# A windowed attention with a SiLU MLP behind it: seven products of quarters in one more group of tokens, and sums of weights that stay on the chip

## Chip, cores and metric

One core of a Trainium2 chip runs the whole program. The metric is device time in microseconds (us) of one launch, median of several runs. The kernel before takes 900.89 us.

## What is computed

Queries, keys and values have 8 batches, 8 heads, 576 positions and 64 columns per head. Attention is causal with a window of 128 positions and a linear bias per head. Its result is laid out as 4608 tokens of 512 columns, `x`, and goes through an MLP:

```
scores = q @ k.T / 8 - slope * distance        (0 <= distance < 128 only)
x      = softmax(scores) @ v                   4608 x 512
h      = x @ w_in                              4608 x 2048
out    = (h * sigmoid(h)) @ w_out              4608 x 512
```

All inputs are float32. The kernel keeps more than float16 precision by splitting each number into a high and a low float16 part and adding three matmuls: high*high, high*low, low*high.

## The kernel before

**Stages.** Tokens go in nine groups of 512, numbered g = 0 to 8 here as in the code (`NG`, `TG`); the "group 7 of nine" of the change's name is g = 6. The hidden width of 2048 is cut in 16 slices of 128 (`NF`), and n = 16*g + f counts group and slice. `gemm1(n, half)` makes a slice of `h`, `act1` to `act4` (L940 to L1009) make SiLU of it and split it in `gh` and `gl`, `gemm2(n, half)` adds its part of the output. Groups 0 and 1 work partly on float32 words; from group 2 on the MLP on TensorE is float16. The attention of later tokens is mixed into the MLP of earlier ones, in "pairs" (one tile of 128 tokens, four heads); nine pairs begin per group until the end of group 6, and groups 7 and 8 run with almost no attention beside them.

**The first and second product of a plain group** (2 to 6): `gemm1` (L897) issues 12 matmuls of 512 columns per slice, `gemm2` (L1114) 4 tiles * 3 = 12 of 512 columns, into the PSUM banks w, x, y, z (one per tile of 128 tokens), which `store` (L1135) empties at the group's end.

**Groups 7 and 8** (`FAST`, L81) work on half a group of tokens (256) and on two slices 1024 columns apart at a time, and take the second product from seven products of quarter matrices instead of eight (`gemm2_fast`, L1017). `gemm1_fast` (L885) issues 2 * 12 matmuls of 256 columns per n, `gemm2_fast` 7 * 3 = 21 of 256 columns. For it ACT and DVE make 7 blocks instead of 4 (`act_sums` L968, `act3` L977, `act4` L996: 896 columns in two instructions instead of 512 in one), and POOL makes sums of the quarters of `w_out` ahead of time (`sum_float`, `sum_make`, `sum_hi`, `sum_lo`, L699 to L744; scheduled from step 302 on, every 17 steps). `join_products` and `add_corners` (L1087, L1068) put the products together from the PSUM banks. In group 8 (`SEVEN`) the first product is taken from seven products too (`gemm1_seven`, L853), with sums of the quarters of `w_in` (`in_float` to `in_lo`, L775 to L796). These are made on POOL and ACT in groups 2 to 4, six of eight are stored to HBM (`in_away`, L756) and loaded again in groups 6 and 7 (`in_back`, L761).

**Order.** The order on each engine is written out by hand. The program is a list of steps; one step is one `gemm1` or `gemm2` half (in group 8 a third of the first product). `plan` holds, by step number, what else is emitted ahead of that step's matmuls: attention, splits, sums. Engines run in that order, and SP's DMA queue issues in it too. `gemm2` of n follows `gemm1` by a lag:

```
left = LAG + (n >= SEVEN * NF - 1) if g in FAST else 1
if f == NF - 1 and (g not in FAST or g == NG - 1):
    left = 0
```

So in plain groups `gemm2` runs one n behind and catches up at the group's end, in groups 7 and 8 it runs 3 behind. A pair p that begins at step n has `scores` at n (PE, into the two PSUM banks a), `row_max` at n+1 (DVE, L526), `exps` at n+2 and n+3 (ACT, L541), `p_hi` (ACT, L551) and `p_lo` (POOL, L557) at n+3 to n+5, a DMA that transposes the halves (`hl`, L567), and `attend` (PE, L609) at n+11, again into a bank a, which `normalize` (DVE, L622 to L638) empties. Pairs begin 7 steps apart.

The scales of batches 4 and 5 and of 6 and 7 come from a chain of four stages (`vscale_finish`, `scales16`, L294), whose last stage is a small matmul on PE (L325). For the last batches the stages stand at steps 268, 271, 273 and 275 (`FINISH`, L66).

Of the kernel before, what the change touches and what calls it, by code (L numbers as in the profile page):

```python
# [121 lines left out]
def tile_window_attention_then_silu_mlp(ctx, tc, qk, v, w_in, w_out, distance, out):  # L122
# [623 lines left out]
    win, piece, away = {}, {}, {}  # L746

    def in_pieces(j):

        both = [pool.tile([P, 2, DM], F32, tag="big", name=f"wb{j}_{k}") for k in range(2)]  # L750
        piece["r"] = [both[0][:, s] for s in range(2)]
        piece["q"] = [both[1][:, s].rearrange("p (s c) -> p s c", s=2) for s in range(2)]
        w = pool.tile([P, 2, 4, DM // 2], F16, tag=IN_TAGS[j] if j < 2 else AWAY[j % 2], bufs=1, name=f"wx{j}")
        win[j] = [w[:, part] for part in range(2)]

    def in_away(j):  # L756
        away[j] = dram.tile([P, 2, 4, DM // 2], F16, name=f"away{j}")
        for part in range(2):
            nc.sync.dma_start(away[j][:, part], win[j][part])

    def in_back(j):  # L761
        if j in IN_TAGS:
            w = pool.tile([P, 2, 4, DM // 2], F16, tag=IN_TAGS[j], bufs=1, name=f"wy{j}")
            win[j] = [w[:, part] for part in range(2)]
        elif j < HALF_F - 1:
            tag, bufs = ("q", 2) if j < 4 else ("x", 4)
            w = [pool.tile([P, 4, DM // 2], F16, tag=tag, bufs=bufs, name=f"wy{j}_{part}") for part in range(2)]
            win[j] = [a[:] for a in w]
        else:
# [11 lines left out]
    def in_make(j, k):
        (a11, a12), (a21, a22) = ([r[:, h * DM // 2 : (h + 1) * DM // 2] for h in range(2)] for r in piece["r"])
        one, two = piece["q"]
        if k == 0:
            nc.gpsimd.tensor_add(one[:, 0], a21, a22)
            nc.gpsimd.tensor_sub(one[:, 1], one[:, 0], a11)
# [300 lines left out]
    def join_products(g, t, half):  # L1087

        scale = gsc[g][:, 2:3]
        if half == 0:  # L1090
            both = pool.tile([P, 2, 2, DM // 2], F32, tag="w1_6", bufs=1, name=f"of{g}_{t}")
            st["out"] = [both[:, k] for k in range(2)]
            st["once"] = once = pool.tile([P, 2, DM // 2], F32, tag="rv", bufs=2, name=f"once{g}_{t}")
            nc.scalar.activation(once.rearrange("p a c -> p (a c)"), ops[1], AF.Copy, scale=scale)
# [445 lines left out]
```

## Time and profile before

| | before |
|---|---|
| median of 3 runs | 900.89 us (900.48 to 901.05) |
| the profiled execution: its time | 901.33 us |
| its span, first to last instruction | 899.5 us |
| PE busy | 99% of the span |
| DVE, ACT, POOL busy | 68%, 68%, 46% |
| group 6 (first matmul of 6 to first of 7) | 644.26 to 741.61 us |
| group 7 (to the first matmul of group 8) | 741.61 to 811.76 us |

The profile records each instruction with its engine, line, tiles and duration. A matmul's duration is its passage through the array, so that neighbours overlap; how fast PE goes is read from the starts of successive blocks. A group of instructions gives the line, the engine, the operation, output<-inputs, the shape, the count, then busy us, mean ns of one, and the idle time of the engine ahead of them with what ended it.

### The profile page before, as it was taken

The numbers are of one execution on the slowest core, as the hardware profiler recorded it, in microseconds if no ns is written. First come the engines' busy times: TensorE is split into PE (matmuls) and PEld (weight loads), VectorE is DVE, ScalarE is ACT, GpSimd is POOL, SyncE is SP. The second block draws the span as 40 slices with busy tenths as digits, with TensorE's granted clock in tenths as the row PEclk, the third lists the DMA queues.
The fourth block names the chain that finished last, engine by engine and source line by source line (L and its number), as shares of the span: only waits on it lengthen the run. The fifth ranks groups of instructions, "written<-read, shape, count | busy, mean of one in ns | idle before, by whom it ended". The sixth has DMA issues, their size and how long they took to land. (4 is left out here: it accounts for less than half of the span.)

```text
span 899.5 us, 20129 instructions
## 1 busy us (share of the span) xinstructions
PE 891.8 (99%) x7657; PEld 592.2 (66%) x7657; DVE 611.3 (68%) x1591; ACT 613.3 (68%) x1336; POOL 411.5 (46%) x462
## 2 busy tenths in 40 slices
PE   9999999999999999999999999999999999999998
PEld 7877777888855555455554454455555558889997
DVE  6998988677866766555766665556665557776665
ACT  7789986776578856878865676656676754435553
POOL 2356652233333326566665775657466721003441
PEclk9999999999999999999999999999999999999999
DMA  8989924345479743878674647343663246310000
GB/s 301 402 204 230 274 56 134 71 94 95 106 205 224 204 95 89 228 175 212 142 176 118 129 106 147 89 96 81 135 145 85 60 107 162 85 37 7 20 26 24
DMA packets 206160, 120.98 MB, mean 134 GB/s; under 512 B 170864, under 2 KB 173040, under 8 KB 206064
## 3 DMA queue, kind: packets, MB, share of 16 engines
q1 hardware_dynamic: 205632, 119.31, 53.1%
q8 instruction: 60, 0.98, 0.5%
q10 hardware_dynamic: 432, 0.39, 0.1%
q14 instruction: 36, 0.29, 0.1%
HBM read 65.67 MB, written 12.58 MB: 87 GB/s over the span
## 5 line engine op out<-in xcount | busy, mean ns | idle before, releaser
L1130 PE MATMUL o<-w,gh 128*128 128x512 f16 (+1 forms) x896 | 273.6, 387 | 0.1
L920 PE MATMUL h<-xt,w 128*128 128x512 f16 (+1 forms) x1344 | 269.7, 349 | 0.0
L557 POOL TENSOR_TENSOR hr<-t,hr 128x512 f16<-128x512 f32 (+1 forms) x108 | 119.7, 1121 | 253.3 <-ACT hr L551 170.7
L920 PEld LDWEIGHTS <-w 128*128 128x128 f16 x1344 | 126.3, 98 | 112.3 <-issue 3.3
L961 DVE SCALAR_TENSOR_TENSOR h<-gt,h 128x512 f32<-128x512 f32 x112 | 77.8, 694 | 159.9 <-ACT gt L955 159.6
L1130 PE MATMUL o<-w,gl 128*128 128x512 f16 (+1 forms) x448 | 172.0, 384 | 0.2
L955 ACT ACTIVATE gt<-h,tsc 128x512 f32<-128x512 f32 x112 | 76.3, 681 | 92.9 <-PE h L920 79.5
L1130 PEld LDWEIGHTS <-gh 128*128 128x128 f16 x640 | 59.3, 98 | 66.7
L526 DVE CUSTOM_DVE_ANT_0 t<-sp,tab 128x256 f32<-128x256 f32 (+1 forms) x288 | 99.9, 401 | 1.9 <-PE sp L502 1.3
L551 ACT ACTIVATE hr<-t 128x512 f16<-128x512 f32 (+1 forms) x128 | 74.1, 598 | 2.6 <-DMA hl<-hr 2.6
L541 ACT ACTIVATE t<-t,mx,vsc 128x256 f32<-128x256 f32 (+1 forms) x144 | 74.8, 578 | 1.2
L1007 DVE SCALAR_TENSOR_TENSOR gl<-h,gh 128x512 f16<-128x512 f32 x80 | 55.0, 687 | 24.2 <-ACT gh L993 23.8
L541 ACT ACTIVATE t<-t,mx 128x256 f32<-128x256 f32 (+1 forms) x144 | 61.8, 488 | 4.5 <-DVE mx L526 3.8
L993 ACT ACTIVATE gh<-h 128x512 f16<-128x512 f32 x80 | 47.2, 590 | 22.4 <-DVE h L961 22.1
L609 PEld LDWEIGHTS <-hl 128*128 128x128 f16 x1464 | 52.0, 98 | 15.8 <-issue 4.5
L171 POOL TENSOR_TENSOR x<-xs,x 128x256 f16<-128x256 f32 x54 | 39.1, 725 | 43.5 <-ACT x L648 43.3
L609 PE MATMUL av<-v,hl 128*128 128x65 f16 (+1 forms) x1464 | 55.4, 193 | 0.9 <-DVE mx L526 0.6
L1130 PEld LDWEIGHTS <-gl 128*128 128x128 f16 x320 | 31.3, 98 | 37.9 <-DVE gl L1007 0.3
L1130 PEld LDWEIGHTS o<-w,gh 128*128 128x128 f32 x256 | 45.6, 188 | 10.0 <-issue 0.5
L925 PE MATMUL h<-xh,w 128*128 128x512 f32 x128 | 44.5, 404 | 0.0
L892 PE MATMUL h<-xt,w 128*128 128x256 f16 x384 | 44.2, 273 | 0.0
L171 POOL TENSOR_TENSOR w<-wm,w 128x512 fp32r<-128x512 f32 x32 | 43.0, 1343 | 2.6
(241 smaller groups left out, 1603.7 us busy)
## 6 DMA issues: line engine op xcount, KB each, us to landing
qs<-qk SPq DMA_DIRECT2D x18, 512.0 KB, 4.8
r<-qk SPq DMA_DIRECT2D x18, 512.0 KB, 4.4
wr<-w_in SPq DMA_DIRECT2D x16, 512.0 KB, 6.6
wr<-w_out SPq DMA_DIRECT2D x16, 512.0 KB, 6.5
rv<-v SPq DMA_DIRECT2D x30, 256.0 KB, 3.5
out<-ot SPq DMA_DIRECT2D x28, 256.0 KB, 3.0
vm<-v SPq DMA_DIRECT2D x27, 256.0 KB, 4.7
q<-qk SPq DMA_DIRECT2D x18, 256.0 KB, 3.9
```

What stands on the lines that cost most here:

```text
L171: engine.tensor_sub(out, a, b)
L526: nc.vector.tensor_tensor_reduce(out=st[p]["t"][u][:, h, 2 * P - n :], in0=st[p]["sp"][h][:, u, o].rearrange("p o c -> p (o c)"), in1=tab[ ...
L541: nc.scalar.activation(x, x, AF.Exp, bias=mx[:, 2 * u + h : 2 * u + h + 1], scale=scale)
L551: nc.scalar.activation(split_of(p, u, hr)[:, 0], t[:, :, 2 * P - n :], AF.Copy, scale=scale)
L557: nc.gpsimd.tensor_sub(hr[:, 1], t[:, :, 2 * P - n :], hr[:, 0])
L609: nc.tensor.matmul(av[:, 2 * u + h, : rhs.shape[-1]], lhs, rhs, start=(n == 0), stop=(n == len(seq) - 1), skip_group_check=True,)
L920: nc.tensor.matmul(o, w[:, wp, cc], x, start=start and k == 0, stop=stop, skip_group_check=True)
L955: nc.scalar.activation(gt, hps[n], AF.Tanh, scale=scale)
L961: nc.vector.scalar_tensor_tensor(out=h, in0=gt, scalar=1.0, in1=h, op0=ALU.add, op1=ALU.mult)
L993: nc.scalar.activation(gh, gt, AF.Copy, scale=cut_of(n))
L1007: nc.vector.scalar_tensor_tensor(out=gl, in0=gt, scalar=cut_of(n), in1=f32(gh) if n // NF < OUT16 else gh, op0=ALU.mult, op1=ALU.subtract)
L1130: nc.tensor.matmul(ops[ti], a[:, t], w, start=(f == 0 and i == 0), stop=(f == NF - 1 and i == len(seq) - 1), skip_group_check=True,)
```

## The change

Seven parts:

1. `FAST` takes in group 6. Its products go through `gemm1_fast` and `gemm2_fast`, its activations through the seven-block form; `act_sums` of group 6 stand on POOL (only those of group 7, `ALONE`, stay on DVE). Its `act3` stands 7 steps behind `gemm1` and its `act4` 8 (`ACT_LATE`, `ACT_LOW`); group 7 keeps 4 and 6.
2. The lag is 1, then 2 from slice 4, then 3 from slice 9 of group 5 (`lag_of`), so that groups 5 and 6 no longer catch up at their ends. Group 5 to 2 put `gh` and `gl` of one n into one tile, tags gh and gl in turn, which gives four n's room.
3. The sums of `w_out` begin at step 176 instead of 302, every 23 steps.
4. The sums of `w_in` for j = 0, 1 stand at steps 191 and 214, those for j = 2 to 7 at 453 to 503, in group 7. `in_away` and `in_back` are gone.
5. For pairs from 18 on, `p_lo` of the second half stands on DVE, `x_hi` and `x_lo` one step later; `v_hi` is two steps earlier and `v_lo` one later, `hi16` and `lo16` move by a step. The sums of x for group 8 are 5 steps later.
6. The four stages of the last scales stand at 268, 274, 281, 288.
7. Outputs of seven-product groups keep their first part in the output tile itself, without the tile `once`; group 6 writes them from two tiles q. Both halves of group 6 and the first half of group 7 add up in banks w, x, y, z; the order of products at a half's start follows.

```diff
-FINISH = {1: (37, 42, 45), 2: (166, 168, 169, 170), 3: (268, 271, 273, 275)}
+FINISH = {1: (37, 42, 45), 2: (166, 168, 169, 170), 3: (268, 274, 281, 288)}
-IN_SUMS = (186, 200, 214, 228, 242, 256, 270, 284)
-IN_BACK = {2: 440, 3: 444, 4: 460, 5: 468, 6: 474, 7: 480}
-AWAY = ("w1_7", "w1_8")
+SUMS, SUMS_STEP = 176, 23
+IN_GAP = 15
+IN_EARLY = (SUMS + IN_GAP, SUMS + SUMS_STEP + IN_GAP)
+IN_FIRST, IN_STEP = 453, 10
+IN_SUMS = IN_EARLY + tuple(IN_FIRST + IN_STEP * j for j in range(8 - len(IN_EARLY)))
-FAST = (NG - 2, NG - 1)
+FAST = (NG - 3, NG - 2, NG - 1)
+ALONE = NG - 2
-SUMS, SUMS_STEP = 302, 17
+RAMP = (4, 9)
+ACT_LATE = 7
+ACT_LOW = 1
+V_HI, V_LO = 7, 3
+P_HI = (3, 4)
+P_LO = (4, 5)
+X_OFF = 3
+LOW_DVE = 1
...
         if p >= LOW_POOL:
-            nc.gpsimd.tensor_sub(hr[:, 1], t[:, :, 2 * P - n :], hr[:, 0])
+            minus(nc.vector if u and LOW_DVE else nc.gpsimd, hr[:, 1], t[:, :, 2 * P - n :], hr[:, 0])
             return
...
-        engine, a = nc.gpsimd if n // NF == SEVEN else nc.vector, gact[n]
+        engine, a = nc.vector if n // NF == ALONE and n % NF >= ALONE_POOL else nc.gpsimd, gact[n]
...
-        gh = pool.tile([P, TG], dt, tag="gh", name=f"gh{n}")
-        gl = pool.tile([P, TG], dt, tag="gl", name=f"gl{n}")
+        if n // NF < OUT16:
+            gh, gl = (pool.tile([P, TG], dt, tag=tag, name=f"{tag}{n}") for tag in ("gh", "gl"))
+        else:
+            both = pool.tile([P, 2, TG], dt, tag=("gh", "gl")[n % 2], name=f"gb{n}")
+            gh, gl = both[:, 0], both[:, 1]
...
-        if j == 0 and g == SEVEN:
+        if j == 0 and g != ALONE:
             first = 3
...
-                    ops[b] = psum.tile([P, DM], F32, tag=("axaz" if t or g == SEVEN else "wxyz")[b], bufs=2 if (t or g == SEVEN) and b % 2 == 0 else 1, name=f"m{g}_{t}_{b}")
+                    free = g == SEVEN or g == ALONE and t
+                    tag = ("axaz" if free else "wxyz")[b]
+                    ops[b] = psum.tile([P, DM], F32, tag=tag, bufs=2 if tag == "a" else 1, name=f"m{g}_{t}_{b}")
...
-        if j > 1:
-            put(IN_SUMS[j] + 17, in_away, j)
-            put(IN_BACK[j], in_back, j)
...
+        def lag_of(n):
+            g, f = divmod(n, NF)
+            if n == NG * NF - 1 or f == NF - 1 and g + 1 < FAST[0]:
+                return 0
+            if g in FAST:
+                return LAG + (n >= SEVEN * NF - 1)
+            return 1 + (f >= RAMP[0]) + (f >= RAMP[1]) if g + 1 in FAST else 1
...
-                left = LAG + (n >= SEVEN * NF - 1) if g in FAST else 1
-                if f == NF - 1 and (g not in FAST or g == NG - 1):
-                    left = 0
+                left = lag_of(n)
```

## Rows read from the trace of the kernel before

**Rows 1.** The page: busy us, share of the span and instructions of each engine.

```profile
PE 891.8 (99%) x7657; PEld 592.2 (66%) x7657; DVE 611.3 (68%) x1591; ACT 613.3 (68%) x1336; POOL 411.5 (46%) x462
```

**Rows 2.** Groups 6 and 7: PE, PEld, DVE, ACT, POOL busy; clock, DMA share, GB/s.

```profile
644.26:741.61 97.35, 97.35 (x817) 49.39 (x816) 54.35 (x157) 64.30 (x127) 56.70 (x63) 1.00 0.47 109
741.61:811.76 70.15, 70.15 (x661) 62.95 (x660) 53.69 (x113) 28.65 (x50) 2.94 (x4) 1.00 0.35 91
```

**Rows 3.** Timeline of PE in group 6: start us, us, engine, line, count.

```profile
702.39 2.75 PE L920 MATMUL h<-xt,w 128*128 128x512 f16 x12
704.98 0.59 PE L1130 MATMUL o<-w,gh 128*128 128x512 f16 x2
```

**Rows 4.** Timeline of PE in group 7.

```profile
764.93 2.78 PE L892 MATMUL h<-xt,w 128*128 128x256 f16 x24
767.55 0.60 PE L1036 MATMUL m<-w,gt 128*128 128x256 f16 x4
...
769.84 2.78 PE L892 MATMUL h<-xt,w 128*128 128x256 f16 x24
```

**Rows 5.** What PE waited for from 250 us on: total us, times, longest.

```profile
PE vs L325 <- DVE mx L526: 0.8, 1, 0.8
PE av L609 <- DMA hl<-hr: 0.2, 1, 0.2
```

**Rows 6.** Timeline at 476 to 480 us, in group 4, the last scales.

```profile
476.72 1.46 PE L920 MATMUL h<-xt,w 128*128 128x512 f16 x6
...
479.00 0.35 PE L325 MATMUL vs<-row,ones 1*128 1x8 f32 x2 [0.82 <-DVE mx L526]
...
479.29 1.47 PE L920 MATMUL h<-xt,w 128*128 128x512 f16 x6
```

**Rows 7.** Groups of instructions by shape, group 6: DVE, ACT and POOL.

```profile
L1007 DVE SCALAR_TENSOR_TENSOR gl<-h,gh 128x512 f16<-128x512 f32 x16 | 11.0, 687 | 4.7 <-ACT gh L993 4.7
L443 DVE SCALAR_TENSOR_TENSOR packed<-r,vsc,packed 128x512 f16<-128x512 f32 x8 | 6.9, 865 | 0.0
...
L993 ACT ACTIVATE gh<-h 128x512 f16<-128x512 f32 x16 | 9.5, 593 | 6.9 <-DVE h L961 6.9
...
L557 POOL TENSOR_TENSOR hr<-t,hr 128x512 f16<-128x512 f32 x19 | 21.8, 1158 | 39.7 <-ACT hr L551 31.1 <-issue 8.3
```

**Rows 8.** The same, group 7: the seven-block split on DVE and on ACT.

```profile
L1000 DVE SCALAR_TENSOR_TENSOR gl<-gt,gh 128x640 f16<-128x640 f32 x7 | 5.7, 818 | 0.2 <-ACT gh L983 0.2
...
L1000 DVE SCALAR_TENSOR_TENSOR gl<-gt,gh 128x256 f16<-128x256 f32 x7 | 2.9, 417 | 0.0
...
L983 ACT ACTIVATE gh<-gt 128x640 f16<-128x640 f32 x7 | 5.1, 735 | 10.2 <-DVE gt L975 10.2
...
L983 ACT ACTIVATE gh<-gt 128x256 f16<-128x256 f32 x7 | 2.8, 400 | 0.0
```

**Rows 9.** POOL's sums over the whole span, by shape.

```profile
L779 POOL TENSOR_TENSOR wb<-w 128x512 f32<-128x512 f16 x16 | 18.9, 1185 | 0.0
...
L973 POOL TENSOR_TENSOR gt<-gt 128x256 f32<-128x256 f32 x7 | 5.1, 729 | 17.7 <-DVE gt L964 17.7
...
L975 POOL TENSOR_TENSOR gt<-gt 128x128 f32<-128x128 f32 x7 | 4.6, 663 | 0.5
```

**Rows 10.** Lines L559 and L443 on DVE: ns min/median/max, first and last start.

```profile
L559 DVE SCALAR_TENSOR_TENSOR hr<-t,hr x20: 669/681/1342, 48.0 to 150.0; 128x512 f16<-128x512 f32 x20
...
L443 DVE SCALAR_TENSOR_TENSOR packed<-r,vsc,packed x36: 731/746/1669, 349.8 to 716.3; 128x512 f16<-128x512 f32 x36
```

**Rows 11.** Timeline of a pair of attention in group 6, and median landing of its transposes.

```profile
698.49 2.27 POOL L557 TENSOR_TENSOR hr<-t,hr 128x512 f16<-128x512 f32 x2 [5.50 <-issue]
...
706.28 0.89 PE L609 MATMUL av<-v,hl 128*128 128x65 f16 x24
...
hl<-hr SPq DMA_TRANSPOSE x18, 2.7
```

**Rows 12.** DMAs that bring sums of w_in back: SP's issue time, ns, first and last.

```profile
L773 SPq DMA_DIRECT2D wy<-away x10: 371/424/533, 733.7 to 762.0; - x10
```

More of the change, by code (lines that the diff above doesn't have):

```diff
@@ L653, in x_lo @@
             cols = slice(q * 4 * D, (q + 1) * 4 * D)
-            minus(nc.gpsimd if p >= LOW_POOL else nc.vector, xt[i][:, 1, cols], st[p]["x"], xt[i][:, 0, cols])
+            minus(nc.gpsimd if p >= LOW_POOL and not X_DVE else nc.vector, xt[i][:, 1, cols], st[p]["x"], xt[i][:, 0, cols])
             if q == 1:
@@ L744, in sum_lo @@
         nc.gpsimd.tensor_sub(out16[:, 1], wsum["r"][:, 0, : DM // 2], out16[:, 0])
[L746 to L769, printed above, removed]
+    win, piece = {}, {}
@@ L770, in in_back, with in_tile @@
+    def in_tile(j):
+        if j == HALF_F - 1:
             flat = [a.rearrange("p s h d -> p (s h d)")[:, : 2 * DM] for a in (v1, v2)]
             win[j] = [a.rearrange("p (s c) -> p s c", s=4) for a in flat]
-        for part in range(2):
-            nc.sync.dma_start(win[j][part], away[j][:, part])
-    def in_float(j, k):
-        if k == 0:
-            in_pieces(j)
-        w = w16[0, j + k * HALF_F]
-        nc.gpsimd.tensor_add(piece["r"][k].rearrange("p (c f) -> p c f", c=NCC), w[:, 0], w[:, 1])
@@ L781, in in_make @@
[L781 to L786, printed above, removed]
-        else:
-            nc.gpsimd.tensor_sub(two[:, 0], a11, a21)
-            nc.gpsimd.tensor_sub(two[:, 1], a12, one[:, 1])
+            return
+        tag, bufs = IN_TAGS[j]
+        if bufs == 1:
+            w = pool.tile([P, 2, 4, DM // 2], F16, tag=tag, bufs=1, name=f"wx{j}")
+            win[j] = [w[:, part] for part in range(2)]
+        else:
+            w = [pool.tile([P, 4, DM // 2], F16, tag=tag, bufs=bufs, name=f"wx{j}_{part}") for part in range(2)]
+            win[j] = [a[:] for a in w]
@@ new lines, in in_float, with in_make @@
+    def in_float(j, k):
+        if j >= len(IN_EARLY):
+            piece[k] = pool.tile([P, DM], F32, tag="rv", bufs=2, name=f"wb{j}_{k}")
+        else:
+            if k == 0:
+                piece["room"] = pool.tile([P, 2, DM], F32, tag=IN_ROOM, bufs=1, name=f"wb{j}")
+            piece[k] = piece["room"][:, k]
+        r = piece[k]
+        w = w16[0, j + k * HALF_F]
+        nc.gpsimd.tensor_add(r.rearrange("p (c f) -> p c f", c=NCC), w[:, 0], w[:, 1])
+    def in_make(j, k):
+        (a11, a12), (a21, a22) = ([piece[k][:, h * DM // 2 : (h + 1) * DM // 2] for h in range(2)] for k in range(2))
+        if k == 0:
+            nc.gpsimd.tensor_add(a22, a21, a22)
+            nc.gpsimd.tensor_sub(a21, a11, a21)
+        else:
+            nc.gpsimd.tensor_sub(a11, a22, a11)
+            nc.gpsimd.tensor_sub(a12, a12, a11)
@@ L1090, in join_products @@
         if half == 0:
[L1091 to L1094, printed above, removed]
+            if g < ALONE:
+                st["out"] = [pool.tile([P, 2, DM // 2], F32, tag="q", bufs=2, name=f"of{g}_{t}_{k}") for k in range(2)]
+            else:
+                both = pool.tile([P, 2, 2, DM // 2], F32, tag="w1_6", bufs=1, name=f"of{g}_{t}")
+                st["out"] = [both[:, k] for k in range(2)]
+            once = st["out"][1]
+            nc.scalar.activation(once, ops[1].rearrange("p (a c) -> p a c", a=2), AF.Copy, scale=scale)
             for k in range(2):
@@ L1099, in join_products @@
             return
-        (corner, other), once = st["out"], st["once"]
+        corner, other = st["out"]
         nc.vector.scalar_tensor_tensor(
-            out=other, in0=ops[0].rearrange("p (a c) -> p a c", a=2), scalar=scale, in1=once, op0=ALU.mult, op1=ALU.add
+            out=other, in0=ops[0].rearrange("p (a c) -> p a c", a=2), scalar=scale, in1=other, op0=ALU.mult, op1=ALU.add
         )
@@ L1288, in tile_window_attention_then_silu_mlp @@
                 put(n + STEP + 1 + u, p_copy_first, p, u)
+        elif not plain:
+            for u in range(2):
+                put(n + P_HI[u], p_hi, p, u)
+                put(n + P_LO[u], p_lo, p, u)
+                put(n + P_LO[u], p_transpose, p, u)
         else:
@@ L1301, in tile_window_attention_then_silu_mlp @@
         put(z + (p < 2 * GT), normalize, p, 1)
-        put(z + 2, x_hi, p)
-        put(z + 2, x_lo, p)
+        put(z + (2 if plain else X_OFF), x_hi, p)
+        put(z + (2 if plain else X_OFF), x_lo, p)
         if q == 0:
@@ L1488, in tile_window_attention_then_silu_mlp @@
                             act1(n)
-                        if n % NF == NF - 1 and not edge:
+                        if n % NF == NF - 1 and g not in FAST and g + 1 not in FAST:
                             turn_over(n)
                         else:
-                            late = 1 if n == 0 else 9 if n == SEVEN * NF - 1 else 11 if n == SEVEN * NF - 2 else 4 if g in FAST and n % NF > 1 else 2
-                            ahead(late + 1 + (late == 4) if n % NF else late, act4, n)
+                            late = 1 if n == 0 else 9 if n == SEVEN * NF - 1 else 11 if n == SEVEN * NF - 2 else ALONE_LATE if g in FAST and n % NF > 1 else 2
+                            if g in FAST and g < ALONE:
+                                late = ACT_LATE
+                            ahead(late + (ACT_LOW if g in FAST and g < ALONE else 1) + (late == ALONE_LATE and g >= ALONE) if n % NF or g in FAST else late, act4, n)
                             ahead(late, act3, n)
```

52 lines of the change are left out of this document (32 added, 20 removed).

## The prediction

> **What bounds the kernel now.** I read the page first. PE is busy 99% of the span; DVE and ACT stand at 68%, POOL at 46% [rows 1]. A busy PE need not be a fast one, so the next view is the timeline of PE. In group 6, 12 matmuls of 512 columns start at 702.39 and the next block at 704.98: 0.216 us each [rows 3]. In group 7, 24 of 256 columns take 764.93 to 767.55 and the 21 behind them 767.55 to 769.84: 0.109 us each [rows 4]. At the upper clock level, 2.4 GHz, 512 columns last 0.213 and 256 last 0.107 us; the granted clock is 1.00, that level, in both stretches [rows 2]. So PE streams columns nearly without a gap, whatever the width. The view of waits agrees: from 250 us on PE stood waiting twice, 1.0 us in all [rows 5]. Only fewer columns, or one of those waits, can save time; any new wait of PE is paid in full.
>
> All durations are from the profiled execution, 901.33 us (span 899.5). It stands 0.44 us above the median of 900.89; I take differences from it and set them against the median. A measurement of this kernel can tell about 0.2%, 1.8 us, from no change.
>
> **Part 1, group 6 by seven products.** A plain slice is 12 + 12 matmuls: 24 * 0.216 = 5.18 us. A slice of group 7 repeats after 769.84 - 764.93 = 4.91 us (45 matmuls of 256 columns) [rows 3, 4]. The difference, 0.27 us, comes 16 times: **-4.3 us**. The attention matmuls of group 6 stay. Bounds: the same columns without any overhead give 768 columns * 16 at 2.4 GHz, -5.1; what the change cannot take away is bounded by PE's waits, below.
>
> Weight loads go with it: 336 more in group 6, each 62.95 / 660 = 0.095 us [rows 2]. PEld rises from 49.4 to 81.4 of about 93 us, 88%. Group 7 has 90% with no gap [rows 2, 5], so I take nothing for it. The Trainium skill ("TensorE: Matmul & The Clock Gate", section "Back-to-back issue gap") speaks against this part: in a stream of weight loads and matmuls it puts a matmul of 128 columns at 81 ns and one of 512 at 131 ns, both operations setting the spacing. An estimate between them, 98 ns for 256 columns, would make group 6 720 * 0.098 - 384 * 0.131 = 20 us longer. The trace does not agree: 216 and 109 ns, half the columns in half the time [rows 3, 4].
>
> **What the seven blocks cost beside PE.** Group 6 shrinks from 97.35 to about 93.0 us.
> - DVE: the split `gl` grows from 0.687 to 0.818 + 0.417 = 1.235 us [rows 7, 8]: 16 times, +8.8. Nine `p_lo` come over, at the 0.681 median of that operation on DVE: +6.1 [rows 10]. Both kinds read two SBUF operands, and with POOL at work such operations stretch: `lo16` takes 0.865 on average in group 6 against its least of 0.731, 1.18 times [rows 7, 10]. With that factor on the new forms DVE goes to 54.35 - 11.0 + 23.3 + 7.2 = 73.9 of 93.0 us, 79%.
> - ACT: `gh` from 0.593 to 0.735 + 0.400 [rows 7, 8]: +8.7, to 73.0 at most (78%), less what the sums of `w_out` used there.
> - POOL: `act_sums` is 2 * 0.729 + 0.663 = 2.12 us [rows 9], 33.9 in all; 9 * 1.158 = 10.4 of `p_lo` go [rows 7], and the last sums of `w_out`. At most 80.2 of 93.0.
>
> No engine passes PE by averages; group 7 ran DVE at 53.69 of 70.15, 77%, and PE waited for nothing [rows 2, 5]. But group 6 has attention beside it. There POOL ends a pair's `p_lo` at 700.76, the transposes take 2.7 us to land, and `attend` starts at 706.28 [rows 11]: 2.8 us of slack per pair. Moving one `p_lo` to DVE takes up to 1.16 us off POOL's stretch, if DVE is not late itself. SP's queue gets two stores per row block in mid-group where none stood; they wait for DVE's joins, and the transposes behind them wait too.
>
> **Bank turnover.** Both halves of group 6 and the first of group 7 use banks w, x, y, z. Ahead of the first matmul into w stand 24 of `gemm1` and nine products (2.62 + 0.98 us), at group 7's start six (2.62 + 0.65). Freeing w takes one DVE add of 512 columns and two of 256, an estimate of 0.69 + 2 * 0.42 = 1.5 us from forms of that size [rows 7, 8]. It is hidden unless DVE is 2 us late.
>
> **New waits of PE.** The trace shows none of these, so I bound them: zero, as in group 7; and, if all new DVE work stretches like the longest `lo16` (1.669 / 0.731 = 2.28) and the longest `p_lo` (1.342) [rows 10], DVE needs 54.35 - 11.0 + 45.1 + 12.1 = 100.5 us, 7.5 over PE. I take **+0.9**, near the lower end, since group 7 at 77% is the nearest row.
>
> **Part 2, the ramp.** It removes no columns. In plain groups the catch-up at the end already costs PE nothing [rows 5]. At the turn from group 5 to 6 the stores have only one slice's `gemm1`, 2.62 us, to empty the first bank; each is one 512-column operation, about 0.7 us. Zero, with the 2 us caveat above.
>
> **Parts 3 to 5.** The sums of `w_in` move six times into group 7: per j four POOL operations of 512 (1.185) and four of 256 (0.729), 7.7 us, every 10 steps of about 1.23 us [rows 4, 9]. POOL was busy 2.94 us there [rows 2]; it fits, and the last ends ahead of its use in group 8. ACT's copies wait for POOL there, with 28.65 of 70.15 us busy. DVE's sums in that stretch read two SBUF operands; at 1.18 its 53.7 us become at most 63, still under 70. Without this room the splits, three slices ahead of PE, would be the first to be late. The DMAs gone (12 out, 12 back; some 0.42 us of SP each [rows 12]) held up no PE instruction. In groups 2 to 5 DVE gains about 8 us per group and POOL loses 10. Zero for all.
>
> **Part 6.** At 476.72 six matmuls start, which need 1.30 us; the next six start at 479.29, and between them the small matmul L325 waited 0.82 us for DVE [rows 6]. Six or more steps between stages end that wait: **-0.9**, bounds -1.0 and 0. Next to be late would be the first user of these scales, two dozen steps on: not soon. **Part 7**: one tile less, the same operations; zero.
>
> **Sum:** -4.3 - 0.9 + 0.9 = -4.3; 900.89 - 4.3 = **896.6 us**.
>
> **Rivals.**
> - *The attention chain turns up late* (chance 0.14). With DVE near 80% and ACT near 75%, a burst eats the 2.8 us of slack and PE waits some 0.3 us for each of nine pairs and 0.5 at three bank turnovers: +4.2 in place of 0.9, 899.9. For it: pairs share in-order queues with larger operations. Against it: `p_lo` is split over two engines, and gh and gl have five steps in hand.
> - *DVE becomes the bound of group 6, and it is slower than before* (0.07). Place: the split and `p_lo` on DVE against `act_sums` on POOL. It decides once DVE needs more than 93 + 7 = 100 us, its new forms stretched about 2.2 times; then 900.89 - 5.2 + 7.5 plus 0.3 us for each of nine pairs late, 905.9. For it: single `lo16` reach 2.28 times [rows 10]. Against: their mean is 1.18 [rows 7].
> - *The saving isn't there* (0.05): PE in group 6 waits at each slice for blocks made by POOL between two DVE and ACT operations, by the 0.27 us that a slice saves. Then -0.9 + 0.9: about 900.9. Against it: five to six steps, 6 us, stand between `act4` and its use.
> - *Weight loads set the pace* (0.01): if the 336 further loads were each unhidden, 336 * 0.095 = +32 us, 929; by the rule weighed above it would be 20 us. Rows 4 leave it hardly a chance.
> - The forecast keeps 0.73.
>
> **Numbers.** Without new waits the time is 895.7, and with the ideal columns 894.9; the upper end takes in the late chain and the case without a saving: 894.9 to 901.2. Faster by over 0.2% (under 899.1): 0.73 plus a part of the late chain, 0.80. Within 0.2%: the rest of that and the missing saving, 0.12. Slower: 0.08.
>
> **What would show it.** PE in group 6 should start blocks of L892 every 4.91 us where no attention stands between; the stretch of group 6 should be near 93 us; PE's waits for L325 gone; DVE near 74 and POOL under 80 us there; POOL near 46 us in group 7. New rows of PE waiting for `hl`, for a bank of the products, or for `gl`, would show the first two rivals. I am wrong if these waits exceed 3 us, or if PE's spacing in group 6 is above 0.110 us.

## The result, and the profile after

The changed kernel takes **914.08 us**, median of 4 runs (913.49 to 916.17); the kernel before took 900.97 on the same chip (900.48 to 902.60). The ratio is 1.0146, interval 1.0126 to 1.0167: slower by 13 us, where 4 us less was forecast. The profiled execution took 913.49 us, its span is 911.7. One of the four executions of e5 below ran at a granted clock of 0.949 and took 920.15 us; it is left out of that kernel's time.

The page of the changed kernel, busy us, share and instructions, to be read against [rows 1]:

```profile
PE 893.5 (98%) x7993; PEld 627.1 (69%) x7993; DVE 682.1 (75%) x1672; ACT 619.4 (68%) x1352; POOL 408.6 (45%) x456
```

PE is hardly busier, DVE by 71 us. Next the stretches, by the first matmul of each group. The ramp moves three slices of `gemm2` from group 5 into 6, so that groups 5 to 7 are compared as one stretch first. Windows of the kernel before, groups 5 to 7 and group 8 (columns as in [rows 2]):

```profile
547.95:811.76 263.81, 263.63 (x2245) 160.43 (x2244) 164.03 (x420) 156.70 (x306) 123.05 (x137) 1.00 0.44 104
811.76:895.62 83.86, 83.86 (x1097) 78.81 (x1094) 54.52 (x105) 45.74 (x119) 31.30 (x45) 1.00 0.04 14
```

The same of the changed kernel, then its groups 6 and 7, and two stretches behind PE's longest waits:

```profile
548.02:822.38 274.36, 263.03 (x2582) 194.08 (x2581) 211.32 (x458) 159.52 (x312) 147.15 (x160) 0.99 0.43 88
822.38:907.77 85.39, 85.39 (x1095) 79.85 (x1094) 59.24 (x114) 46.87 (x121) 34.69 (x48) 0.98 0.04 14
...
635.48:733.25 97.77, 95.17 (x1129) 79.84 (x1126) 75.38 (x185) 64.54 (x129) 57.54 (x70) 1.00 0.55 112
733.25:822.38 89.13, 80.40 (x752) 70.55 (x749) 81.22 (x126) 37.90 (x68) 54.18 (x52) 0.98 0.26 46
...
791.00:795.00 4.00, 3.64 (x19) 2.63 (x19) 3.10 (x8) 1.69 (x3) 1.56 (x3) 0.57 0.00 0
...
820.00:825.00 5.00, 2.62 (x19) 2.23 (x19) 4.02 (x10) 1.74 (x4) 3.05 (x5) 0.72 0.00 0
```

Up to group 5 the kernels stand level (548.02 and 547.95). Groups 5 to 7 then take 10.6 us more, group 8 takes 1.5 more. In group 7 PE is idle for 89.13 - 80.40 = 8.7 us, with DVE busy 81.2 of 89.1 us. What PE waited for from 250 us on, most of it there, against the two entries of [rows 5]:

```profile
PE h L874 <- DVE gt L975: 5.0, 1, 5.0
PE m L1052 <- DVE io L1014: 2.1, 2, 1.7
PE av L627 <- DMA hl<-hr: 2.0, 4, 0.8
PE m L1052 <- DVE of L1095: 1.1, 1, 1.1
PE vs L343 <- DVE row L340: 0.5, 1, 0.5
```

Those of the products and of group 8's start are nearly all waits for DVE: for a split (L1014), a join (L1095), and, ahead of group 8, for the SiLU itself (L975). The groups of DVE in group 7 by shape say why it is late; they answer to [rows 8] and [rows 9] (`act_sums` is L984 to L986 here, the split L1014):

```profile
L985 DVE TENSOR_TENSOR gt<-gt 128x256 f32<-128x256 f32 x14 | 12.2, 871 | 0.0
L975 DVE SCALAR_TENSOR_TENSOR gt<-gt,h 128x512 f32<-128x512 f32 x15 | 10.2, 682 | 4.2 <-ACT gt L966 4.2
L986 DVE TENSOR_TENSOR gt<-gt 128x128 f32<-128x128 f32 x14 | 8.2, 588 | 0.5
L1014 DVE SCALAR_TENSOR_TENSOR gl<-gt,gh 128x640 f16<-128x640 f32 x8 | 8.0, 1001 | 0.8 <-ACT gh L994 0.8
...
L1014 DVE SCALAR_TENSOR_TENSOR gl<-gt,gh 128x256 f16<-128x256 f32 x8 | 5.4, 680 | 0.0
```

L975 reads `h` from PSUM and lasts 682 ns, against 687 for the same operation in that group of the kernel before. The forms with two SBUF inputs have grown: 128x640 from 818 to 1001 ns, 128x256 of the split from 417 to 680. The timeline shows it happen. DVE around 810 and 815 us:

```profile
808.96 0.69 DVE L975 SCALAR_TENSOR_TENSOR gt<-gt,h 128x512 f32<-128x512 f32 x1 [0.84 <-ACT gt L966]
809.68 0.42 DVE L984 TENSOR_TENSOR gt<-gt 128x256 f32<-128x256 f32 x1
810.02 0.41 DVE L985 TENSOR_TENSOR gt<-gt 128x256 f32<-128x256 f32 x1
810.47 0.29 DVE L986 TENSOR_TENSOR gt<-gt 128x128 f32<-128x128 f32 x1
...
814.53 1.26 DVE L984 TENSOR_TENSOR gt<-gt 128x256 f32<-128x256 f32 x1
815.72 1.37 DVE L985 TENSOR_TENSOR gt<-gt 128x256 f32<-128x256 f32 x1
817.12 1.12 DVE L986 TENSOR_TENSOR gt<-gt 128x128 f32<-128x128 f32 x1
```

and POOL in the same microseconds, idle until 814.36, then with the sums of `w_in`:

```profile
814.36 2.45 POOL L807 TENSOR_TENSOR wx<-wb,wx 128x512 f16<-128x512 f32 x2 [6.52 <-ACT wx L803]
816.77 2.49 POOL L789 TENSOR_TENSOR wb<-w 128x512 f32<-128x512 f16 x2
```

With POOL idle the three sums take 0.42, 0.41 and 0.29 us. Beside POOL they take 1.26, 1.37 and 1.12: each about as long as one of POOL's instructions (2.45 / 2 = 1.2), whatever its own length. The ends fit too: POOL's second L807 ends at 814.36 + 2.45 = 816.81, and L985, begun at 815.72, ends 0.28 us later. PE pays behind it; its timeline:

```profile
822.38 0.80 PE L874 MATMUL h<-xt,w 128*128 128x128 f16 x6 [4.99 <-DVE gt L975]
...
823.61 1.06 PE L1052 MATMUL m<-w,gh 128*128 128x256 f16 x4
824.46 1.06 PE L1052 MATMUL m<-ws,gh 128*128 128x256 f16 x4
```

Four matmuls of 256 columns go from 823.61 to 824.46, 0.213 us each, twice the 0.109 of [rows 4]: the granted clock from 820 to 825 is 0.72 on average, part of it at the lower level of 1.2 GHz, after PE had stood idle for 5.0 us. Likewise 0.57 from 791 to 795, after waits of 1.75 and 0.36 us.

### The profile page after: what moved, and what is told of

It reads as the page before. It is cut to its first block, busy times and chain, and to the rows that moved or that the text cites. A ratio compares the mean times of both kernels' runs of the same rounds, so it can differ in the third digit from the quotient of the medians.

```text
span 911.7 us, 20873 instructions
## 1 busy us (share of the span) xinstructions
PE 893.5 (98%) x7993; PEld 627.1 (69%) x7993; DVE 682.1 (75%) x1672; ACT 619.4 (68%) x1352; POOL 408.6 (45%) x456
## 4 chain that ended last, share of the span: by engine, by line
PE 77%; DVE 13%; ACT 5%; issue 2%; POOL 1%; DMA 1%; SPq 0%; DVEq 0%; ACTq 0%; POOLq 0%
PE o L1149 25%; PE h L931 21%; PE m L1052 6%; PE h L936 4%; PE av L627 4%; PE sp L520 4%; PE h L903 2%; PE h L874 2%; PE sp L513 2%; PE hb L874 2%; DVE io L1014 1%; PE av L614 1%; DVE gl L1014 1%; DVE gt L975 1%; ACT gt L966 1%
## 5 line engine op out<-in xcount | busy, mean ns | idle before, releaser
L931 PE MATMUL h<-xt,w 128*128 128x512 f16 (+1 forms) x1152 | 224.2, 344 | 0.0
L1149 PE MATMUL o<-w,gb 128*128 128x512 f16 x768 | 179.5, 379 | 0.1
L931 PEld LDWEIGHTS <-w 128*128 128x128 f16 x1152 | 108.5, 98 | 91.6 <-issue 3.3
L966 ACT ACTIVATE gt<-h,tsc 128x512 f32<-128x512 f32 x112 | 76.4, 682 | 108.9 <-PE h L931 73.9
L189 POOL TENSOR_TENSOR hr<-t,hr 128x512 f16<-128x512 f32 (+1 forms) x54 | 63.3, 1173 | 184.7 <-issue 81.1
L1149 PEld LDWEIGHTS <-gb 128*128 128x128 f16 x768 | 72.1, 98 | 83.6 <-DVE gb L1021 1.2
L189 POOL TENSOR_TENSOR x<-xs,x 128x256 f16<-128x256 f32 x54 | 39.3, 728 | 129.1 <-ACT x L666 129.1
L903 PE MATMUL h<-xt,w 128*128 128x256 f16 x768 | 90.5, 274 | 0.0
L1149 PE MATMUL o<-w,gh 128*128 128x512 f32 x256 | 83.0, 405 | 0.4 <-ACT gh L1003 0.4
L903 PEld LDWEIGHTS <-w 128*128 128x128 f16 x768 | 74.6, 98 | 9.6
L559 ACT ACTIVATE t<-t,mx,vsc 128x256 f32<-128x256 f32 (+1 forms) x144 | 75.1, 578 | 1.2
L569 ACT ACTIVATE hr<-t 128x512 f16<-128x512 f32 (+1 forms) x128 | 74.4, 597 | 1.8 <-DMA hl<-hr 1.8
L559 ACT ACTIVATE t<-t,mx 128x256 f32<-128x256 f32 (+1 forms) x144 | 61.8, 488 | 4.7 <-DVE mx L544 4.0
L1021 DVE SCALAR_TENSOR_TENSOR gb<-h,gb 128x512 f16<-128x512 f32 x64 | 43.9, 686 | 16.4 <-ACT gb L1007 16.2
L1149 PE MATMUL o<-w,gl 128*128 128x512 f32 x128 | 50.8, 397 | 0.2
L191 DVE SCALAR_TENSOR_TENSOR hr<-t,hr 128x512 f16<-128x512 f32 (+1 forms) x54 | 43.5, 805 | 4.0 <-ACT hr L569 3.8
```

The source lines that it names most:

```text
L189: engine.tensor_sub(out, a, b)
L559: nc.scalar.activation(x, x, AF.Exp, bias=mx[:, 2 * u + h : 2 * u + h + 1], scale=scale)
L569: nc.scalar.activation(split_of(p, u, hr)[:, 0], t[:, :, 2 * P - n :], AF.Copy, scale=scale)
L903: nc.tensor.matmul(out, w[:, wp, cc], xt[g, "g"][:, 2 * t : 2 * t + 2, xp * NCC + cc], start=half == 0 and i == 0, stop=i == len(seq) - 1, ...
L931: nc.tensor.matmul(o, w[:, wp, cc], x, start=start and k == 0, stop=stop, skip_group_check=True)
L966: nc.scalar.activation(gt, hps[n], AF.Tanh, scale=scale)
```

## The experiments

The letters are those of the expectations. **A**: six sums of `w_in` on POOL beside DVE's sums and splits in group 7 make DVE late, and this is the loss. Rivals: group 6's seven products cost it, or (**C**) ACT's queue, whose `in_hi` copies wait for POOL ahead of the activations. Unless another kernel is named, diffs are against the changed kernel.

### e1: the late sums left out

This kernel makes no sums for j = 2 to 7 and uses those of j = 0 and 1 in their place.

```diff
-    for j in range(HALF_F):
+    for j in range(len(IN_EARLY)):
...
-            return win[j][part][:, k, cc * P : (cc + 1) * P]
+            return win[j % 2][part][:, k, cc * P : (cc + 1) * P]
```

> Leaves out the sums of w_in for j = 2 to 7 (POOL, ACT and their waits in group 7); group 8 multiplies with the sums of j = 0 and 1 in their place, so the amount of PE work is the same. Theory A (POOL's sums make DVE's operations on two SBUF operands wait, DVE becomes the bound of group 7, PE waits there and at the start of group 8): about 914 - 10 = 904 us, L985 on DVE back to 0.42 us mean from 0.81, no 5.0 us wait ahead of group 8, group 7 from 89 to 81 us. Rival B (the turn-over of banks and the lag, not the sums): above 911. Rival C (ACT stands behind copies that wait for POOL): also about 904, so it is told from A by the next run.

901.36 us, ratio 0.9998 (0.9989 to 1.0007). Windows of groups 6, 7 and of 5 to 7:

```profile
637.24:735.30 98.06, 95.40 (x1130) 79.88 (x1126) 75.31 (x185) 64.52 (x129) 57.50 (x70) 1.00 0.56 111
735.30:813.06 77.76, 77.76 (x751) 69.86 (x748) 61.99 (x134) 32.78 (x58) 4.72 (x6) 1.00 0.26 53
...
549.78:813.06 263.28, 260.62 (x2581) 193.41 (x2580) 192.03 (x467) 154.38 (x302) 97.64 (x114) 1.00 0.44 92
```

and DVE's forms in group 7:

```profile
L985 DVE TENSOR_TENSOR gt<-gt 128x256 f32<-128x256 f32 x15 | 6.3, 419 | 0.0
L986 DVE TENSOR_TENSOR gt<-gt 128x128 f32<-128x128 f32 x15 | 4.4, 292 | 0.5
```

The late sums cost 914.08 - 901.36 = 12.7 us: all of the loss. Group 7 falls from 89.13 to 77.76 us, PE waits for nothing there, DVE's sums are back at 0.42 and 0.29. The second reading matters as much: without the late sums the kernel is no faster than before. Groups 5 to 7 take 263.28 us against 263.81, so of the 4.3 us of part 1 only 0.5 show in the stretch. From 250 us on PE waits here for these:

```profile
PE av L627 <- DMA hl<-hr: 2.2, 4, 0.8
...
PE av L627 <- DVE v L494: 0.5, 1, 0.5
```

2.7 us of waits of the attention, where before had 0.2 [rows 5].

### e2: the late sums on POOL alone

ACT's copies for j = 2 to 7 are left out. POOL runs the same number of sums without them, and group 8 uses those of j = 0 and 1.

```diff
     def in_hi(j, k):
+        if j >= len(IN_EARLY):
+            return
...
+        r = piece[k].rearrange("p (s c) -> p s c", s=2)
-        nc.gpsimd.tensor_sub(lo, piece[k].rearrange("p (s c) -> p s c", s=2), hi)
+        nc.gpsimd.tensor_sub(lo, r, hi if j < len(IN_EARLY) else r)
...
-            return win[j][part][:, k, cc * P : (cc + 1) * P]
+            return win[j % 2][part][:, k, cc * P : (cc + 1) * P]
```

> As the changed kernel, but ACT's copies of the late sums of w_in are left out; POOL does the same number and shape of operations (its low halves are made from the sums alone, and group 8 multiplies with the sums of j = 0 and 1). Theory A: POOL still stretches DVE, 911 to 914 us, with L985 on DVE at 0.7 us or more. Rival C (ACT's queue held by copies that wait for POOL): 903 to 906 us.

917.98 us, ratio 1.0180 (1.0163 to 1.0196). Group 7's window:

```profile
733.66:827.99 94.33, 81.72 (x751) 69.87 (x748) 87.04 (x133) 32.89 (x58) 57.38 (x54) 0.98 0.21 43
```

C falls: with ACT out of it POOL no longer waits for ACT's copies (21.2 us ahead of L807 in the changed kernel), its sums follow each other more closely, and DVE is busy 92% of a longer group. The time is 4 us above what A allowed for.

### e3: group 6 plain, the late sums kept

```diff
-FAST = (NG - 3, NG - 2, NG - 1)
+FAST = (NG - 2, NG - 1)
...
-OUT_TAGS = {3: ("q", 2), 4: ("q", 2), 5: ("q", 2)}
+OUT_TAGS = {3: ("q", 2), 4: ("q", 2), 5: ("q", 2), 6: ("q", 2)}
```

> Group 6 takes its second product in the plain way again; all else of the change stays (the ramp now stands in group 6). Theory A: group 7's wait stays, group 6 gets 4.3 us of columns back and loses its own waits of about 4.8 us: 912 to 915 us. Rival D (the seven products in group 6 cause the lateness that group 7 inherits): 903 us or less.

914.76 us, ratio 1.0143 (1.0127 to 1.0158), with the same 5.0 us wait ahead of group 8. So group 6's seven products don't cause the loss. No gain of theirs can be measured either: the changed kernel stands at 1.0146 (1.0126 to 1.0167), and its groups 5 to 7 take 274.36 us against 274.14 here, by the starts of the groups.

### e4: all sums of w_in early

The sums go back to steps 186 to 277, six through HBM with the functions of the kernel before, every 13 steps; those of `w_out` follow from 286 on, every 12, in 9 steps each instead of 14.

```diff
-SUMS, SUMS_STEP = 176, 23
+SUMS, SUMS_STEP = 286, 12
...
+IN_SUMS = tuple(186 + 13 * j for j in range(8))
+IN_BACK = {2: 440, 3: 466, 4: 460, 5: 468, 6: 474, 7: 480}
```

> Undoes the sums on chip alone: all sums of w_in are made early again (steps 186 to 277), six of eight go to HBM and back; the sums of w_out follow at steps 286 to 370. Group 6 keeps its seven products. Theory A: group 7 without POOL's sums takes about 81 us again, the total is 900.9 - 5.2 + 4.8 (group 6's own waits) = 900 to 902 us. Rival D: above 908.

903.05 us, ratio 1.0011 (1.0002 to 1.0021): the whole computation, and 11 of the 13 us are back. Group 7 takes 77.76 us again. It is 1 us more than A's upper end; group 5, where the sums of `w_out` now end, takes 90.3 us instead of the changed kernel's 87.5.

### e5: three late, five early

j = 2, 3 and 4 are made before group 6 and go through HBM; 5, 6 and 7 stay in group 7, 15 steps apart.

```diff
-IN_SUMS = IN_EARLY + tuple(IN_FIRST + IN_STEP * j for j in range(8 - len(IN_EARLY)))
+IN_SUMS = IN_EARLY + (260, 283, 306) + (453, 468, 483)
```

> Only three of the sums of w_in (j = 5, 6, 7) stay in group 7, 15 steps apart; j = 2, 3, 4 are made at steps 260 to 306, go to HBM and come back. Theory A (the cost comes only once DVE has no room left): DVE busy in group 7 about 70 of 78 us and no wait of PE there: 900.5 to 902.5 us, what remains are group 6's own waits. Against A: if half of the sums cost half of the 13 us, about 908.

905.37 us (median of three), ratio 1.0044 (1.0027 to 1.0061): 4.0 of the 12.7 us above e1, between what A and the rule of halves gave. A's forecast that PE would not wait in group 7 is missed: in e7, which has the same three late sums, PE waits there for joins, 2.2 us in two places, and group 7 takes 80.47 us, 2.7 more than in e1. Nor is group 4 free, where the other three now stand: 100.15 us in e7 against 98.33 in the changed kernel. The next three kernels start from this one.

### e6: e5, and group 6's split two steps earlier

Theory E: group 6's own waits come of its splits standing too late.

```diff
-ACT_LATE = 7
+ACT_LATE = 5
```

> As e5_half_late, with the two splits of group 6 two steps earlier (ACT_LATE 5 in place of 7). Group 6's four late transposes are 4 us of PE's waits. Theory E (two tiles for the seven blocks tie ACT's tanh of slice n+2 to DVE's split of slice n, and ACT's queue with its exps and p_hi stands behind it): the split comes earlier, the waits fall, 898 to 900 us. Rival F (DVE, ACT and POOL simply have too much two-operand work beside attention): no gain or a loss, since the same work only moves, 900.5 to 903.

911.40 us, ratio 1.0108 (1.0093 to 1.0123), beyond both theories. E falls, with the opposite sign: group 6 takes 104.2 us (638.50 to 742.65), and PE waits there 2.3 us for a store of group 5 at the turn (the caveat of the prediction's part 2) and 1.3 for row maxima, both on DVE, and still 2.0 for `hl`. One reading, not tried by itself: the splits now stand in the queues of DVE and ACT and wait for POOL's `act_sums`, with the stores and the attention behind them.

### e7: e5, and a third tile for gt in group 6

Before it the tanh of n + 2 (ACT) waits for the split of n (DVE), because two tiles hold `gt`. The sum of `w_in` for j = 1 goes through HBM too, which frees the third tile.

```diff
-                gt = pool.tile([P, 2 * TG], F32, tag="big", name=f"gt{n}")
+                tag, bufs = ("w1_3", 1) if n // NF < ALONE and n % 3 == 2 else ("big", 2)
+                gt = pool.tile([P, 2 * TG], F32, tag=tag, bufs=bufs, name=f"gt{n}")
```

> As e5_half_late, with a third tile for the seven blocks in group 6 (the room of w_in's sum 1, which goes to HBM and back). Theory E: ACT's waits for DVE's split ahead of the tanh (L966) vanish from group 6 (4.7 us in e1_no_late_sums) and PE's waits for transposes with them, 897 to 899 us. Rival F: ACT's waits vanish, but PE still waits 3 to 4 us for transposes: 900 to 902.

905.26 us, ratio 1.0034 (1.0021 to 1.0047): the interval overlaps that of e5, so no gain is shown. ACT's waits for the split are gone from group 6 (4.7 us for `gl` in e1), which takes 96.54 us; PE still waits 1.7 us for `hl` in four places. E falls here too.

### e8: e5, and POOL's and DVE's work of group 6 swapped

Theory F: the load of DVE decides in group 6 too. `act_sums` go to DVE, all `p_lo` to POOL (from pair 18 on, so the groups before 6 are touched as well).

```diff
-LOW_DVE = 1
+LOW_DVE = 0
...
-        engine, a = nc.vector if n // NF == ALONE and n % NF >= ALONE_POOL else nc.gpsimd, gact[n]
+        engine, a = nc.vector if n // NF <= ALONE else nc.gpsimd, gact[n]
```

> As e5_half_late, with act_sums of group 6 on DVE and both p_lo on POOL (as group 7 and the kernel before have them). DVE then needs some 11 us more in group 6 (16 * 1.16 less 9 * 0.83), POOL 23 us less (34 less 10.4), and POOL's p_lo no longer stands behind act_sums that wait for DVE. Theory F (load of DVE and contention decide): DVE at 90%, PE waits longer, above 903. Theory E says little: about 901. Rival G (POOL's order: p_lo queued behind act_sums that wait for DVE) would gain: 898 to 900.

921.04 us, ratio 1.0213 (1.0196 to 1.0230). Group 6's window, and PE's longest waits in the whole span, most of them in group 6:

```profile
641.19:748.73 107.54, 97.72 (x1129) 80.93 (x1126) 82.51 (x220) 62.83 (x127) 31.50 (x30) 0.98 0.50 99
```

```profile
PE sp L515 <- DVE xs L658: 4.0, 3, 1.9
PE av L629 <- DVE mx L546: 3.4, 3, 2.6
PE av L629 <- DVE v L496: 3.4, 4, 1.0
```

F holds: DVE gets 7 us more than the changed kernel's 75.38 and group 6 becomes 9.8 us longer, with POOL busy 31.5 us of it. The change's choice of POOL for `act_sums` was right.

### e9 and e10: six early, two late, p_lo on POOL

From e7: six sums early, two late, `p_lo` on DVE only in the last pairs, `w_out`'s sums between, and the stages of batch 2's scales spread. Theory G, in e9 alone (the last two cuts of the diff): `act_sums` of group 6 two steps later keep POOL's queue from standing behind DVE.

```diff
-FINISH = {1: (37, 42, 45), 2: (166, 168, 169, 170), 3: (268, 274, 281, 288)}
+FINISH = {1: (37, 42, 45), 2: (166, 168, 171, 174), 3: (268, 274, 281, 288)}
...
-SUMS, SUMS_STEP = 176, 23
+SUMS, SUMS_STEP = 264, 14
...
+IN_SUMS = tuple(186 + 13 * j for j in range(6)) + (460, 478)
...
-            minus(nc.vector if u and LOW_DVE else nc.gpsimd, hr[:, 1], t[:, :, 2 * P - n :], hr[:, 0])
+            minus(nc.vector if u and LOW_DVE and p >= 62 else nc.gpsimd, hr[:, 1], t[:, :, 2 * P - n :], hr[:, 0])
...
-        act_sums(n)
+        if n // NF >= ALONE:
+            act_sums(n)
...
+                                if g in FAST and g < ALONE:
+                                    ahead(3, act_sums, n)
```

> A version meant to beat both: the change, with w_in's sums at steps 186 to 251 (five of eight to HBM and back) and only two in group 7, w_out's sums at steps 264 to 375, the second p_lo on DVE from pair 62 on only, the third tile for the seven blocks of group 6, and act_sums of group 6 emitted two steps after act2, so that POOL's queue does not stand behind DVE ahead of p_lo. Theory A: group 7 near 78 us, groups 2 to 5 without new waits. Theory G (POOL's p_lo behind act_sums that wait for DVE makes the transposes of group 6 late): group 6's waits under 1.5 us, 896.5 to 898.5 us.

> As e9_spread_delayed with act_sums directly behind act2, as in the changed kernel. Theory G: 2 to 3 us slower than e9, PE's waits for transposes in group 6 near 2.5 us again, POOL's waits for DVE ahead of act_sums about 30 us in group 6 as in e1 and less than 15 in e9. Rival F: the two are equal within 0.7 us, and both keep group 6's waits of 2.5 to 4 us (898 to 900).

913.40 us, ratio 1.0131 (1.0114 to 1.0148), and 912.58, ratio 1.0126 (1.0111 to 1.0141): both expectations of the time are missed, and G gains nothing. What G says of POOL's queue does come true in group 6: POOL waits 4.1 us for DVE ahead of `act_sums` in e9 against 31.0 in e10, and PE's waits for `hl` there, 1.4 us in e10, are gone. In their place PE waits 1.7 us for operations of DVE itself (1.2 for `xs`, 0.5 for `mx`), and the group takes 96.3 us against 95.8. Groups 6 and 7 are as short as in e7 (95.8 and 79.5 us in e10), but group 3 is not. e10's window of it:

```profile
353.08:456.80 103.72, 97.28 (x770) 47.93 (x769) 52.78 (x152) 78.08 (x178) 64.93 (x69) 1.00 0.69 188
```

It took 96.1 us in the kernel before, by the starts of its groups. PE waits for the attention there. The load of POOL alone doesn't explain it: the kernel before has all `p_lo` and sums of `w_in` on POOL in that group too, busy for 62.4 us against 64.9, and PE waits for nothing. Which of the edits does it was not taken apart.

### e11: e4 with a third tile and batch 2's scales spread

The sum of `w_in` for j = 1 goes through HBM too, as in e7. Against e4:

```diff
-FINISH = {1: (37, 42, 45), 2: (166, 168, 169, 170), 3: (268, 274, 281, 288)}
+FINISH = {1: (37, 42, 45), 2: (166, 168, 171, 174), 3: (268, 274, 281, 288)}
...
-                gt = pool.tile([P, 2 * TG], F32, tag="big", name=f"gt{n}")
+                tag, bufs = ("w1_3", 1) if n // NF < ALONE and n % 3 == 2 else ("big", 2)
+                gt = pool.tile([P, 2 * TG], F32, tag=tag, bufs=bufs, name=f"gt{n}")
```

> As e4_early_sums (all of w_in's sums made before group 6, five or six of them through HBM), with two more edits: a third tile for gt in group 6 (w_in's j=1 goes through HBM too, so that w1_3 is free), and FINISH's entry of batch 2 spread to steps 166, 168, 171, 174. Theory A (the late sums beside VectorE's sums in group 7 are what cost the 12.7 us; the rest is small waits, each with its own cause): group 6, 97.07 us in e4, loses the waits that come of two tiles, as in e7_third_tile, about 1 us, to 96; group 7 stays at 77.8; the waits of group 5 (1.7 and 1.0 us, w_out's sums squeezed) stay. Time about 901.5 us, 0.999 to 1.002 of before. Rival (the seven products of group 7 themselves cost what they save, wherever the sums are made): 903 us or more, as e4.

901.94 us, ratio 1.0003 (0.9994 to 1.0012). Its windows of groups 6 and 7, then PE's waits from 250 us on:

```profile
638.40:734.90 96.50, 94.50 (x1129) 79.78 (x1126) 77.09 (x187) 64.81 (x131) 59.66 (x72) 1.00 0.54 113
734.90:812.66 77.76, 77.76 (x751) 69.82 (x748) 61.98 (x134) 32.77 (x58) 4.74 (x6) 1.00 0.38 100
```

```profile
PE av L625 <- DMA hl<-hr: 3.0, 3, 1.4
PE av L625 <- DVE v L492: 0.7, 1, 0.7
PE av L625 <- DVE mx L542: 0.3, 1, 0.3
```

As A says, within the bounds. It is the quickest kernel with seven products in group 6 that does the whole computation, and it is no faster than the kernel before. The 0.5 us that PE waits at the scales of batch 2 in e4 (L341) are gone with their stages spread. Attention makes PE wait 4.0 us: 2.0 in group 6 (96.50 - 94.50), the rest in group 5, beside which the sums of `w_out` now end.

### e12: the kernel before with part 6 alone

```diff
-FINISH = {1: (37, 42, 45), 2: (166, 168, 169, 170), 3: (268, 271, 273, 275)}
+FINISH = {1: (37, 42, 45), 2: (166, 168, 169, 170), 3: (268, 274, 281, 288)}
```

> The kernel before with one number group of the change alone: the steps of batch 3's scale work spread from 268, 271, 273, 275 to 268, 274, 281, 288. What the prediction said of it (its part 6): the 0.82 us wait of TensorE for the scales near 477.8 us goes, nothing takes its place, time 0.9 us down, about 900.1 us (0.999). Rival: as in the changed kernel, where the same wait was gone but one of 0.5 us for the scales of batch 2 stood near 317.9 us: if that wait comes of the spread too, 900.6 us; if it comes of the other parts, 900.1.

901.31 us, ratio 0.9998 (0.9989 to 1.0006): no gain that can be measured. Group 4, where these stages stand, takes 99.2 us, 99.0 before. The timeline of PE, at the two stages of these scales that stand on PE:

```profile
478.26 0.49 PE L303 MATMUL vt<-ident,vcol 128*1 128x128 f32 x3 [0.41 <-DVE mx L526]
...
500.59 0.35 PE L325 MATMUL vs<-row,ones 1*128 1x8 f32 x2 [0.50 <-DVE mx L526]
```

The wait of 0.82 us [rows 6] has become two, 0.91 together. In both cases PE waits at a small matmul of the scales for a DVE operation that comes late (the profile names `mx`, the row maximum in the same queue); spreading divides the wait.

## Why the prediction was wrong

**The step that failed: "Parts 3 to 5. ... Zero for all."** It costed POOL's late sums by POOL's own time ("it fits") and DVE's stretch by a factor: "at 1.18 its 53.7 us become at most 63, still under 70". Two faults.
- The factor came from `lo16`, an operation of 512 columns. The stretch is no factor. In the timeline above it is the rest of POOL's instruction, which DVE sits out. On average that is +0.45 us on a sum of 256 columns (871 against e1's 419) and +0.30 on one of 128 (588 against 292), both doubled, but the sums are not alike (ns, least/median/most, group 7):

```profile
L985 DVE TENSOR_TENSOR gt<-gt x14: 412/947/1374, 737.9 to 815.7; 128x256 f32<-128x256 f32 x14
...
L986 DVE TENSOR_TENSOR gt<-gt x14: 291/293/1126, 738.3 to 817.1; 128x128 f32<-128x128 f32 x14
```

  At least half of the 128-column sums lose nothing, and the longest loses 0.83 us, nearly the 0.96 of the longest 256-column sum. So short operations suffer most, and group 7 is full of them. DVE went from 61.99 us (e1) to 81.22, 19.2 us more; the prediction allowed 9.
- The base was too low. 53.7 us is group 7 of before; the changed one holds more of it between its first matmuls, 61.99 of 77.76 us in e1. The room was 16 us, 19 were taken.

The Trainium skill has this rule ("SBUF — State Buffer", section "SBUF: two separate sides"): one pair of SBUF ports is shared by DVE and GpSimd, which is POOL here, and an operation that takes it, on DVE one with two SBUF inputs, holds it for the whole instruction while the other blocks. The trace agrees: L984, L985 and L986 take 1.26, 1.37 and 1.12 us beside POOL, L975 with its PSUM input keeps 0.68. The rule should have been weighed against "it fits".

**Rival 2 had the mechanism, in the wrong group.** It let DVE become the bound by stretched forms, at 905.9 us, and placed that in group 6 at a stretch of 2.2; the sums themselves reached 2.1 (871 / 419) in group 7. Its price lacked the clock: after the idle stretches PE ran part of the time at 1.2 GHz. Of the 11.4 us that group 7 lost against e1, 8.7 are idle time of PE and 80.40 - 77.76 = 2.6 more busy time, the slower matmuls among it; group 8 lost 1.5 more.

**"New waits of PE", +0.9: mis-sized.** In group 6 the view of waits has 2.7 us in e1 (98.06 - 95.40) and 2.0 in e11, nearly all of the attention behind its transposes, which is the first rival (+4.2). The reason given, group 7 as the nearest row, was no good one: it has almost no attention. DVE in group 6 was busy 75.38 us (73.9 forecast), but of 97.8 us, not 93.0. How its lateness reaches PE, in a pair of the changed kernel (L569 and L189 make `hr`, which is transposed into `hl`):

```profile
717.77 0.62 ACT L569 ACTIVATE hr<-t 128x512 f16<-128x512 f32 x1
...
720.09 0.73 POOL L984 TENSOR_TENSOR gt<-gt 128x256 f32<-128x256 f32 x1 [2.60 <-DVE r L645]
...
722.90 1.34 POOL L189 TENSOR_TENSOR hr<-t,hr 128x512 f16<-128x512 f32 x1
...
727.06 0.53 PE L627 MATMUL av<-v,hl 128*128 128x65 f16 x12 [0.39 <-DMA hl<-hr]
728.40 0.54 PE L627 MATMUL av<-v,hl 128*128 128x65 f16 x12 [0.81 <-DMA hl<-hr]
```

ACT's half is ready at 718.39, but POOL's `p_lo` begins at 722.90: it stands in POOL's queue behind the three `act_sums`, and these behind a wait of 2.60 us for DVE. The transposes follow, and PE waits twice. This is what e9 took away in group 6, and there PE waited for DVE elsewhere instead. The wait of 0.74 us at 643.73 in e1 is of another kind: there SP took 3.69 us to issue one transpose (637.17), three times the usual 1.23; why stays open.

These waits cost more than the view of waits says. The 12 matmuls from 727.06 on start some 0.03 us apart, so that 728.40 is about 1.0 us late, but a matmul's passage of 0.19 us still counts as busy. Added up from the starts of all matmuls in groups 5 to 7, PE stands still 4.0 us in e1 and 0.3 in the kernel before: 3.6 us where 0.9 was forecast.

**Part 1, -4.3: right, but the attention takes it back.** PE in group 6 of the changed kernel, where no attention stands between:

```profile
660.00 2.78 PE L903 MATMUL h<-xt,w 128*128 128x256 f16 x24
662.62 0.60 PE L1052 MATMUL m<-w,gt 128*128 128x256 f16 x4
```

24 matmuls in 2.62 us, 0.109 each, as in [rows 4]. Weight loads set no pace (PEld 79.84 of 97.77 us in group 6). Counted by starts, with the waits taken out, the products of groups 5 to 7 take 232.8 us in e1 and 237.1 in the kernel before: the 4.3 us are there. Less the 3.6 of the waits above, 0.7 should be left, and e1's stretch is 0.5 shorter.

**Part 6, -0.9: wrong that nothing is late next.** Alone, in e12, the part gains nothing. In the changed kernel the wait at 479 is gone and group 4 is 0.6 us shorter (98.33 against 98.96), so there it works in part. The 0.5 us at the scales of batch 2 (L343) stand in group 2, ahead of the steps that this part moves, and e12 has only 0.2 us there: they come in the main of another part.

**Part 2 and part 7 at zero: not contradicted.** Up to group 5 both kernels stand within 0.1 us, and none of PE's waits of the changed kernel lies in the ramp.

## What to carry to other kernels

Before filling an idle POOL, ask what DVE does in that stretch: for each DVE operation with two SBUF inputs allow the rest of a POOL instruction, not a percentage, and compare with DVE's room there. A saving on the engine at 99% is only worth what its neighbours' slack lets through; count the slack in the stage that the saving shortens, against the stage's new length. Work that is moved to an engine also stands in that engine's queue: what it waits for, everything behind it waits for. And a wait that seems cheap to spread may just divide.

## What had not been expected of the hardware

- A DVE sum of 128 columns, 0.29 us alone, took 1.12 us beside POOL, nearly as long as one of 256 columns (1.26 and 1.37). POOL suffers as well: its 128x256 sums took 1.09 us on average at L794, against 0.73 for that shape in [rows 9].
- PE's granted clock fell after waits of 1.75 and 0.36 us (0.57 from 791 to 795), and a stretch at 1.2 GHz makes a late stage later still.
